# Values' products of an attention kernel, divided over the two row halves of the array

## The chip, the cores and the metric

The kernel runs on one core of a Trainium2 chip. The core has five engines, each with an instruction queue of its own that is worked off in order: TensorE (PE; its weight loads are shown apart, as PEld), VectorE (DVE), ScalarE (ACT), GpSimd (POOL) and SyncE (SP), which issues most of the DMAs. They wait for each other through semaphores. Matrix products are written to the eight banks of PSUM, 128 partitions by 512 float32 numbers each; everything else lies in SBUF. The metric is the device time of one execution in microseconds, and less is better.

## The reference

Two independent attentions over 2048 positions, model width 576, 32 heads of 18. A is local: every query sees itself and seven earlier positions, two apart. B is full softmax attention. Their outputs stand side by side in the result.

```python
qkv = (x @ wqkv).reshape(B, S, 3, H, Dh).transpose(2, 0, 3, 1, 4)
q, k, v = qkv[0], qkv[1], qkv[2]
# A: W, dil = 8, 2
logits = jnp.einsum("bhsd,bhswd->bhsw", q, kg) * scale      # kg, vg: eight gathered neighbours
o = jnp.einsum("bhsw,bhswd->bhsd", softmax(logits), vg)
# B
scores = jnp.einsum("bhqd,bhkd->bhqk", q, k) * scale
o = jnp.einsum("bhqk,bhkd->bhqd", softmax(scores), v)
# both
return o.transpose(0, 2, 1, 3).reshape(B, S, D) @ wo
```

## The kernel before

**Stages.** First come the projections of both attentions, then the main loop over B's attention with A's work strewn in, then a tail in which output projections are finished. TensorE's float32 inputs are split in a high and a low part where accuracy asks for it, so that projections are sums of several products.

**B's attention.** The heads are taken in 8 groups of 4 (NG = 8), the queries in 4 blocks of 512 (NB = 4), the keys in 16 steps of 128 (NT = 16). A step of the main loop (from "while step < ALL" on) handles 128 keys of 4 heads for 512 queries, and there are 8 x 4 x 16 = 512 steps. In a step `score` (lines 259 to 277) is called four times, for heads 0, 2, 1, 3. It multiplies 56 rows, in the upper half of the array's rows for heads 0 and 2 (r = 0) and the lower half for 1 and 3 (r = 1), into one score bank (L269), and ScalarE takes the exponential into a tile e in SBUF (L276). The product of e with the values is `weigh` (L736 to L742). It runs one step later: in step n, behind the four scores of step n, come the values of step n - 1. Each of the four heads has 18 value columns and a column of ones for the denominator, 19 columns; the four heads' results lie at partitions 0, 32, 64 and 96 of one bank, po, and add up there over the block's 16 steps.

**Maxima.** Softmax needs a bound of the scores. For blocks to come, the scores are computed in the other direction (queries on partitions) and VectorE takes maxima over the keys: `take` (the product, L158) and `reduce` (L166). The order of a step is written out by hand at the end of the kernel: half a maximum for r = 1, score 0, a maximum for r = 1, score 2, score 1, half a maximum for r = 0, score 3, a maximum for r = 0, then the values. In steps whose number is in `copied` the half maxima are left out.

**Banks.** Seven banks beside po are handed out by `bank` in rings. In the main loop the ring "scores" has banks 0 to 3 and serves the scores in turn; the ring "else" has banks 4, 5, 6 and serves the maxima. Sums of A's output projection (`sums_of_a`, `beside`, L1058) take one bank of either ring. A bank is used again when its last reader has ended.

**Tiles e.** There are eight, six in one pool and two in another, used in turn by `counted`; a tile is written again when the values' products that read it have ended.

**A block's end.** When the 16th step's values are issued, `finish` (L744) copies po to a tile o in SBUF: on ScalarE (L749) where the next step holds a sum of A (`producing`) or no maxima are left, else on VectorE (L752). From there, steps later and through `later`: the denominators go out by DMA on SP's queue (step +1), VectorE inverts them (+8, L777), they are spread by DMA, and GpSimd multiplies o with them (+20, L780) and splits it (+21, +22). `later` and `plan` fix the place in the program's order; when it runs, each engine decides by its queue and its waits. For the last group the tail does this in a shorter way (`shortly`), and for the very last block `closing` (L817) works on po in two halves of columns.

**A's attention** is done on GpSimd (L882, L886, L925 to L928), a little on VectorE and ScalarE, planned over the steps by `local`.

**The tail.** When the maxima are used up, values are weighed for two steps together (`paired`), and sums of B's output projection stand between.

The loop's order, cut to what the change touches:

```python
for h in (0, 2, 1, 3):
    es[h] = score(g, b, kt, h, ...)
    ...
if ready and (kt % 2 == 0 or not paired):
    weigh(ready.pop(0))
ready.append((g, b, kt, es))
```

Of the kernel before, what the change touches and what calls it, by code (L numbers as in the profile page):

```python
# [7 lines left out]
F32 = mybir.dt.float32  # L8
F32R = mybir.dt.float32r
BF16 = mybir.dt.bfloat16  # L10
AF = mybir.ActivationFunctionType
# [12 lines left out]
NT = S // 128  # L24
NB = S // 512
SCALE = DH ** -0.5
# [22 lines left out]
def ap(t, *dims):  # L49

    return bass.AP(tensor=t.tensor, offset=t.offset, ap=[list(t.ap[0])] + [list(d) for d in dims])


def rows(t, *dims):

    return bass.AP(tensor=t.tensor, offset=t.offset, ap=[list(d) for d in dims])
# [3 lines left out]
def two_attentions(ctx: ExitStack, tc, xa, wa, woa, xb, wb, wob, out):  # L60
# [5 lines left out]
    nc = tc.nc  # L66
# [6 lines left out]
    p_bank = ctx.enter_context(tc.tile_pool(name="p_bank", bufs=1, space=PSUM))  # L73
# [3 lines left out]
    rings = {"all": list(range(7)), "scores": [0, 1, 2, 3], "else": [4, 5, 6]}  # L77
    ring = "all"

    def bank(kind=None):  # L80
        r = rings[kind or ring]
        r.append(r.pop(0))
        return p_bank.tile([128, 512], F32, name=f"bank{r[-1]}")
# [11 lines left out]
    po = p_po.tile([128, 512], F32, name="po")  # L95
# [10 lines left out]
    step = 0  # L106
# [4 lines left out]
    def plan(start, pieces):  # L111
        for n, f in pieces:
            agenda[start + n].append(f)
# [100 lines left out]
    given = [0, 0]  # L214
# [44 lines left out]
    e_room = None  # L259
    counted = [-1]  # L260

    def score(g, b, kt, h, kind="scores", between=None):

        assert (g, b) in placed
        qs, ks = sets[g % 3]
        p, r = divmod(h, 2)
        ps = bank(kind)
        at = slice(64 * r, 64 * r + 56)
        nc.tensor.matmul(ps, ks[at, p, 128 * kt : 128 * kt + 128], qs[at, b, p], start=True, stop=True)  # L269
        if between:  # L270
            between()

        counted[0] += 1
        early = counted[0] % 8 < 6
        e = (e_room if early else work).tile([128, 512], F32, name="e", bufs=6 if early else 2)
        nc.scalar.activation(e, ps, AF.Exp, scale=SCALE)  # L276
        return e

    vs = {}

# [97 lines left out]
    with (tc.tile_pool(name="x", bufs=1, side="right") as xp,  # L378
# [4 lines left out]
        early = ExitStack()  # L383
# [98 lines left out]
        if True:  # L482
# [34 lines left out]
            for c in range(5):  # L517
                one, other = (load, nc.scalar.dma_start) if c % 2 == 0 else (nc.scalar.dma_start, load)
# [79 lines left out]
            for t in range(NT):  # L598
                ps = bank()
# [94 lines left out]
            for t in order[:4]:  # L694
                ps = bank()
# [23 lines left out]
            es = []  # L719
# [10 lines left out]
        step = 0  # L730
# [2 lines left out]

    work = ctx.enter_context(tc.tile_pool(name="work", bufs=1, reuse_waits="tile"))
    ring = "else"
    def weigh(*steps):  # L736
        for g, b, kt, es in steps:
            for i in range(4):
                nc.tensor.matmul(po[32 * i : 32 * i + 19], vs[g][:, kt, 19 * i : 19 * i + 19], es[i],  # L739
                                 start=kt == 0, stop=kt == NT - 1)  # L740
        if kt == NT - 1:
            finish(g, b)  # L742

    def finish(g, b):  # L744
        o = work.tile([128, 512], F32, name="o", bufs=2)
        if g == NG - 1 and b == NB - 1:
            return closing(b, o, work.tile([128, 512], F32, name="rec", bufs=1))
        if step + 1 in producing or sum(given) == total:
            nc.scalar.activation(o, po, AF.Copy)  # L749
        else:  # L750

            nc.vector.tensor_copy(o, po)  # L752
            copied.add(step + 1)
        den = work.tile([128, 16], F32, name="den", bufs=2)
        rec = work.tile([128, 512], F32, name="rec", bufs=1)
        parts = []

        def room():
            if g == NG - 1 and b == 0:

                parts[:] = [ap(work.tile([128, 4, 128], F32R, name=f"at{i}", bufs=1), (1, 512)) for i in range(2)]
            else:
                n = work.tile([128, 2, 512], F32R, name="n", bufs=1)
                parts[:] = n[:, 0], n[:, 1], n
            return parts

        if g == NG - 1 and b > 0:
            return shortly(b, o, rec, *room()[:2])

        def store():  # L770
            if g < NG - 1:
                load(do[:, g, :, 512 * b : 512 * b + 512].rearrange("i p n -> p i n"), parts[2].bitcast(F32))
            else:
                plan(step, full(b, parts))

        for at, f in ((1, lambda: load(den, o[DH:128:32])),
                      (8, lambda: nc.vector.reciprocal(den, den)),  # L777
                      (9, lambda: load(drec[g, b].rearrange("i (p n) -> (i p) n", n=16), den)),
                      (13, lambda: load(rec, rows(drec[g, b], (512, 4), (0, 32), (1, 512)))),
                      (20, lambda: nc.gpsimd.tensor_mul(o, o, rec)),  # L780
                      (21, lambda: nc.gpsimd.tensor_copy(room()[0], o)),
                      (22, lambda: nc.gpsimd.tensor_sub(parts[1], o, parts[0])),
                      (26, store)):
            later(at, f)

    def shortly(b, o, rec, hi, lo):

        def halved(cols):
            nc.gpsimd.tensor_copy(hi[:, cols], o[:, cols])
            nc.gpsimd.tensor_sub(lo[:, cols], o[:, cols], hi[:, cols])  # L790


        cols = [slice(256 * i, 256 * i + 256) for i in range(2)]
        apart = b == 1
        for i in range(2):
            later(1 + i * apart, lambda i=i: nc.vector.transpose(rec[:, cols[i]], o[:, cols[i]]))
        later(1 + 2 * apart, lambda: divided(rec))
        for i in range(2):
            later(1 + (3 + i) * apart, lambda i=i: nc.vector.transpose(o[:, cols[i]], rec[:, cols[i]]))
            later(1 + (3 + i) * apart, lambda i=i: halved(cols[i]))  # L800
        plan(step, [(at + 2, f) for at, f in full(b, (hi, lo))])

    def inverse(src, turned, cols, o):

        nc.vector.transpose(turned[:, cols], src[:, cols])
        divided(turned[:, cols])
        nc.vector.transpose(o[:, cols], turned[:, cols])
# [9 lines left out]
    def closing(b, o, rec):  # L817

        n = work.tile([128, 2, 512], F32R, name="n", bufs=1)
        first(3, b, 1)  # L820
        for t in range(4):
            if t % 2 == 0:
                inverse(po, rec, slice(128 * t, 128 * t + 256), o)
            cols = slice(128 * t, 128 * t + 128)
            hi, lo = n[:, 0, cols], n[:, 1, cols]
            nc.scalar.activation(hi, o[:, cols], AF.Copy)
            nc.gpsimd.tensor_sub(lo, o[:, cols], hi)
        for t in range(4):
            end(t, b, (n[:, 0], n[:, 1]))
# [4 lines left out]
    producing = set()  # L834
# [322 lines left out]
    early = sum(given)  # L1157
    rest = NG * NB * PIECES * 2 - early

    total = early + rest  # L1160
# [4 lines left out]
    while step < ALL:  # L1165
        n, kt = divmod(step, NT)
        g, b = divmod(n, NB)
        es = [None] * 4
# [4 lines left out]
        ps = bank() if inside and whole else None  # L1173
# [60 lines left out]
```

## Time and profile before

| | |
|---|---|
| time, median of 3 runs | 1605.34 us (1602.68 to 1605.59) |
| span of the profiled execution | 1603.8 us |
| TensorE, VectorE, ScalarE, GpSimd busy | 1590.0, 1383.7, 1217.7, 960.1 us |
| granted clock of TensorE, mean | 0.998 |
| 4096 records of the values' products (L739) | 537.7 us busy |
| 2048 records of the scores (L269) | 568.9 us busy |
| 2048 exponentials (L276) | 1049.9 us busy |
| 2048 maxima (L166) | 1288.3 us busy |

The runs' times are of unprofiled executions; the span is that of the one that was profiled, from its first to its last instruction. Busy time counts overlapping instructions of an engine once. In the profile a line such as L739 is a line of the kernel; "po<-e,v" names the tile that is written and those that are read; "128*19 128x512" on TensorE means 128 rows of the array, 19 columns, 512 numbers streamed. "x8" is a count. In the groups, the two numbers after the bar are the busy time in us and the mean duration in ns, then comes the engine's idle time before such instructions and what ended it. In a timeline the columns are start and duration in us; a row with a count reaches from the first start to the last end. Ends of matmuls are modelled.

### The profile page before, as it was taken

The numbers are of one execution on the slowest core, as the hardware profiler recorded it, in microseconds if no ns is written. First come the engines' busy times: TensorE is split into PE (matmuls) and PEld (weight loads), VectorE is DVE, ScalarE is ACT, GpSimd is POOL, SyncE is SP. The second block draws the span as 40 slices with busy tenths as digits, with TensorE's granted clock in tenths as the row PEclk, the third lists the DMA queues.
The fourth block names the chain that finished last, engine by engine and source line by source line (L and its number), as shares of the span: only waits on it lengthen the run. The fifth ranks groups of instructions, "written<-read, shape, count | busy, mean of one in ns | idle before, by whom it ended". The sixth has DMA issues, their size and how long they took to land.

```text
span 1603.8 us, 35232 instructions
## 1 busy us (share of the span) xinstructions
PE 1590.0 (99%) x13388; PEld 950.3 (59%) x13388; DVE 1383.7 (86%) x2347; ACT 1217.7 (76%) x2438; POOL 960.1 (60%) x792
## 2 busy tenths in 40 slices
PE   9999999999999999999999999999999999999998
PEld 7999888999543444444444444444444444445676
DVE  5299899999999999999999999999999999999512
ACT  6423441221699999999999999999999999898655
POOL 2405742201166995896797897797797797772100
PEclk9999999999999999999999999999999999999999
DMA  8937954522312362254326325422632231144111
GB/s 247 235 125 199 258 173 124 162 92 80 74 37 67 72 143 72 59 133 99 73 76 143 74 78 131 105 78 61 135 100 65 65 96 32 50 163 157 62 39 60
DMA packets 186058, 172.11 MB, mean 107 GB/s; under 512 B 119152, under 2 KB 132976, under 8 KB 184160
## 3 DMA queue, kind: packets, MB, share of 16 engines
q1 hardware_dynamic: 181024, 158.31, 36.1%
q0 software_dynamic: 4032, 10.63, 3.1%
q8 instruction: 105, 1.72, 0.5%
q10 hardware_dynamic: 832, 0.92, 0.2%
q14 instruction: 65, 0.53, 0.1%
HBM read 96.94 MB, written 71.90 MB: 105 GB/s over the span
## 4 chain that ended last, share of the span: by engine, by line
PE 91%; DVE 4%; DMA 2%; ACT 2%; issue 0%; POOL 0%; SPq 0%; POOLq 0%; DVEq 0%; ACTq 0%
PE po L739 29%; PE bank L269 18%; PE bank L158 17%; PE bank L361 15%; PE bank L1058 8%; PE bank L298 5%; DVE mx L166 3%; ACT e L276 1%; DMA dqk<-olo 1%; DMA dqk<-ohi 1%; DMA den<-o 0%; POOL xlo L409 0%; PE bank L513 0%; DVE as L900 0%; ACT lg L909 0%
## 5 line engine op out<-in xcount | busy, mean ns | idle before, releaser
L166 DVE TENSOR_REDUCE mx<-bank 128x2 f32<-128x512 f32 x2048 | 1288.3, 684 | 110.5 <-PE bank L158 82.6
L276 ACT ACTIVATE e<-bank 128x512 f32<-128x512 f32 x2048 | 1049.9, 608 | 46.6 <-PE bank L269 43.3
L158 PE MATMUL bank<-ks,qs 54*128 54x256 f32 (+1 forms) x2530 | 787.7, 378 | 4.2 <-DVE mx L166 2.5
L158 PEld LDWEIGHTS bank<-ks,qs 54*128 54x128 f32 x2530 | 408.8, 184 | 445.7 <-DVE mx L166 397.0
L269 PE MATMUL bank<-qs,ks 56*128 56x512 f32 x2048 | 568.9, 426 | 0.0
L739 PE MATMUL po<-e,v 128*19 128x512 f32 x4096 | 537.7, 599 | 0.0
L269 PEld LDWEIGHTS bank<-qs,ks 56*128 56x128 f32 x2048 | 299.7, 184 | 29.3 <-ACT e L276 25.2
L882 POOL TENSOR_TENSOR pr<-aq,akv 128x1024 f32<-128x1024 f32 x72 | 158.3, 2200 | 15.8 <-DMA akv<-da 13.0
L925 POOL TENSOR_TENSOR pr<-lg,akv 128x1024 f32<-128x1024 f32 x72 | 158.3, 2199 | 0.6
L886 POOL TENSOR_TENSOR pr<-pr 128x1024 f32<-128x1024 f32 x64 | 152.6, 2384 | 5.0
L739 PEld LDWEIGHTS po<-e,v 128*19 128x19 f32 x4096 | 70.5, 97 | 129.1 <-issue 123.6
L689 ACT ACTIVATE ohi<-bank 128x512 f32<-128x512 f32 (+1 forms) x56 | 30.4, 595 | 150.8 <-issue 104.2
L361 PE MATMUL bank<-xhi,ahi 64*128 64x512 f32 (+1 forms) x448 | 114.3, 387 | 0.0
L361 PE MATMUL bank<-xhi,alo 64*128 64x512 f32 (+1 forms) x448 | 109.6, 387 | 0.0
L361 PE MATMUL bank<-xlo,ahi 64*128 64x512 f32 (+1 forms) x448 | 105.8, 388 | 0.1
L926 POOL TENSOR_TENSOR pr<-pr 128x512 f32<-128x512 f32 x72 | 92.4, 1284 | 5.6
L409 POOL TENSOR_TENSOR alo<-raw,ahi 128x512 fp32r<-128x512 f32 (+1 forms) x14 | 17.6, 1255 | 121.4 <-ACT ahi L408 113.2
L501 POOL TENSOR_TENSOR olo<-olo,ohi 128x512 fp32r<-128x512 f32 x36 | 46.2, 1294 | 70.9 <-ACT ohi L500 62.8
L101 POOL CAST mh<-mt 128x32 fp32r<-128x32 f32 x32 | 6.7, 210 | 101.5 <-DVE mt L183 96.3
L361 PEld LDWEIGHTS bank<-xhi,ahi 64*128 64x128 f32 (+1 forms) x448 | 64.1, 182 | 4.4
L499 ACT ACTIVATE olo<-bank 128x512 f32<-128x512 f32 x36 | 21.2, 589 | 56.4 <-PE bank L361 31.4
L361 PEld LDWEIGHTS bank<-xhi,alo 64*128 64x128 f32 (+1 forms) x448 | 60.2, 182 | 4.4
(203 smaller groups left out, 1846.2 us busy)
## 6 DMA issues: line engine op xcount, KB each, us to landing
do<-n SPq DMA_DIRECT2D x28, 512.0 KB
da<-ohi SPq DMA_DIRECT2D x52, 256.0 KB
akv<-da SPq DMA_DIRECT2D x64, 175.5 KB
out<-y SPq DMA_DIRECT2D x32, 288.0 KB
qs<-dqk SPq DMA_DIRECT2D x30, 288.0 KB
ks<-dqk SPq DMA_DIRECT2D x30, 288.0 KB
at<-dao SPq DMA_DIRECT2D x60, 128.0 KB
rec<-drec SPq DMA_DIRECT2D x29, 256.0 KB
```

Source lines behind the costliest of these rows:

```text
L158: return nc.tensor.matmul(ps if part is None else ps[:, 256 * r : 256 * r + 256], qs[at, b, p, 128 * t : 128 * t + 128], ks[at, p, 512 * k ...
L166: nc.vector.tensor_reduce(at, ps.rearrange("q (s n) -> q s n", s=2), axis=AX.X, op=ALU.max)
L269: nc.tensor.matmul(ps, ks[at, p, 128 * kt : 128 * kt + 128], qs[at, b, p], start=True, stop=True)
L276: nc.scalar.activation(e, ps, AF.Exp, scale=SCALE)
L298: nc.tensor.matmul(ps, a, b, start=c == i == 0, stop=c == 4 and i == 1)
L361: nc.tensor.matmul(ps, a, b, start=start, stop=stop)
L739: nc.tensor.matmul(po[32 * i : 32 * i + 19], vs[g][:, kt, 19 * i : 19 * i + 19], es[i], start=kt == 0, stop=kt == NT - 1)
L882: nc.gpsimd.tensor_mul(pr, ap(st["q"][:, 2 * c], (SUB, 2), (0, W), (1, SUB)), window(st["k"], c))
L886: nc.gpsimd.tensor_add(st["pr"], st["pr"], pr)
L925: nc.gpsimd.tensor_mul(at, ap(st["lg"], (0, 2), (SUB, W), (1, SUB)), window(st["v"], c))
L926: nc.gpsimd.tensor_add(at[:, :, :4], at[:, :, :4], at[:, :, 4:])
L1058: nc.tensor.matmul(ps, a, b, start=start, stop=stop)
```

## The change

Every values' product over 128 keys is divided in two products of 64 keys, one in either half of the array's rows. The upper half's results add up in po, the lower half's in a second bank, po2, which is bank 3 of the score ring; three banks are left for the scores. At a block's end ScalarE copies po2 to a tile taken from the e tiles' turn, VectorE copies po, and GpSimd adds the two. The very last block adds them with VectorE, half by half.

```diff
@@ in score
+        e = room_of_e()
+        nc.scalar.activation(e, ps, AF.Exp, scale=SCALE)
+        return e
+
+    def room_of_e():
         counted[0] += 1
         early = counted[0] % 8 < 6
-        e = (e_room if early else work).tile([128, 512], F32, name="e", bufs=6 if early else 2)
-        nc.scalar.activation(e, ps, AF.Exp, scale=SCALE)
-        return e
+        return (e_room if early else work).tile([128, 512], F32, name="e", bufs=6 if early else 2)
@@ before the main loop
+    rings["scores"].remove(3)
+    po2 = p_bank.tile([128, 512], F32, name="bank3")
+    nc.vector.memset(po2, 0.0)
+
     def weigh(*steps):
         for g, b, kt, es in steps:
             for i in range(4):
-                nc.tensor.matmul(po[32 * i : 32 * i + 19], vs[g][:, kt, 19 * i : 19 * i + 19], es[i],
-                                 start=kt == 0, stop=kt == NT - 1)
+                for r, to in enumerate((po, po2)):
+                    at = slice(64 * r, 64 * r + 64)
+                    nc.tensor.matmul(to[32 * i : 32 * i + 19], vs[g][at, kt, 19 * i : 19 * i + 19], es[i][at],
+                                     start=kt == 0, stop=kt == NT - 1)
@@ in finish
-        if step + 1 in producing or sum(given) == total:
-            nc.scalar.activation(o, po, AF.Copy)
-        else:
-
-            nc.vector.tensor_copy(o, po)
+        other = room_of_e()
+        nc.scalar.activation(other, po2, AF.Copy)
+        nc.vector.tensor_copy(o, po)
+        if not (step + 1 in producing or sum(given) == total):
             copied.add(step + 1)
+        nc.gpsimd.tensor_add(o, o, other)
@@ in closing
         for t in range(4):
             if t % 2 == 0:
-                inverse(po, rec, slice(128 * t, 128 * t + 256), o)
+                both = slice(128 * t, 128 * t + 256)
+                nc.scalar.activation(o[:, both], po2[:, both], AF.Copy)
+                nc.vector.tensor_add(o[:, both], po[:, both], o[:, both])
+                inverse(o, rec, both, o)
```

## The prediction

> **What bounds the kernel now.** I read the page first, for the engines and the chain that ended last.
>
> ```profile
> span 1603.8 us, 35232 instructions
> ...
> PE 1590.0 (99%) x13388; PEld 950.3 (59%) x13388; DVE 1383.7 (86%) x2347; ACT 1217.7 (76%) x2438; POOL 960.1 (60%) x792
> ...
> PE 91%; DVE 4%; DMA 2%; ACT 2%; issue 0%; POOL 0%; SPq 0%; POOLq 0%; DVEq 0%; ACTq 0%
> ```
>
> TensorE looks like the only bound, but its ends are modelled, so I ask the stages. Columns: us, then busy us of PE, PEld, DVE, ACT and POOL, then granted clock and DMA.
>
> ```profile
> 700.00:1000.00 300.00, 299.57 (x2473) 139.29 (x2474) 280.94 (x480) 285.82 (x566) 246.37 (x176) 1.00 0.42 100
> 1500.00:1604.00 104.00, 97.82 (x1106) 72.60 (x1098) 23.22 (x55) 56.45 (x122) 4.48 (x10) 0.99 0.12 44
> ```
>
> In the attention stage ScalarE is 95% busy, VectorE 94%, GpSimd 82%: three engines stand beside TensorE, at a full clock, so time freed on TensorE alone is worth little there unless the others can follow. Only the last hundred microseconds are TensorE's alone. Next, one step of the loop (128 keys of 4 heads) in the timeline, a row for each group.
>
> ```profile
> 801.41 0.63 PE L739 MATMUL po<-e,v 128*19 128x512 f32 x4
> 801.85 0.61 PE L739 MATMUL po<-e,v 128*19 128x512 f32 x4
> 802.36 0.62 ACT L276 ACTIVATE e<-bank 128x512 f32<-128x512 f32 x1
> 802.39 0.38 PE L158 MATMUL bank<-ks,qs 54*128 54x256 f32 x1
> 802.40 0.50 PE L269 MATMUL bank<-qs,ks 56*128 56x512 f32 x1
> 802.93 0.60 ACT L276 ACTIVATE e<-bank 128x512 f32<-128x512 f32 x1
> 803.03 0.18 PEld L269 LDWEIGHTS bank<-qs,ks 56*128 56x128 f32 x1
> 803.08 0.46 PE L269 MATMUL bank<-qs,ks 56*128 56x512 f32 x1
> 803.10 0.43 PE L158 MATMUL bank<-ks,qs 54*128 54x512 f32 x1
> 803.47 0.63 PE L739 MATMUL po<-e,v 128*19 128x512 f32 x4
> 804.45 0.38 PE L158 MATMUL bank<-ks,qs 54*128 54x256 f32 x1
> ```
>
> Values at 801.41 and again at 803.47: a step is 2.06 here. A float32 values' product shows as two records, so the four products are eight: four at 801.41, four at 801.85. Two joints are idle. The last maximum starts at 803.10 and the values only at 803.47, 0.37 later; the values start at 803.47 and the next score phase at 804.45, 0.98 later. The first joint is seen in the waits too:
>
> ```profile
> PEld po L739 <- issue: 110.9, 452, 0.3
> PEld bank L269 <- ACT e L276: 22.8, 43, 0.8
> ```
>
> 452 times, 0.25 us each, a weight load of the values waited for nothing that the profile names: the array emptying between 128-row and 64-row products. The second thing to see is the fourth score of the step (803.08). Its weight load stands at 803.03, just after the exponential that ended at 802.36 + 0.62 = 802.98: that one frees the score bank which the ring of four gives it. The loop is tied to ScalarE through the banks.
>
> **The change part by part.**
>
> *Products in halves.* Eight products (sixteen records) of 64 rows by 19 columns replace four of 128 by 19. Does the joint go? The page has no 64x19 product, but one neighbour: the last projection chunk runs 64 rows by 64 columns among 64-by-128 maxima.
>
> ```profile
> 419.29 0.39 PE L361 MATMUL bank<-xhi,ahi 64*64 64x512 f32 x1
> 419.30 0.39 PE L361 MATMUL bank<-xhi,alo 64*64 64x512 f32 x1
> 419.52 0.39 PE L158 MATMUL bank<-ks,qs 54*128 54x512 f32 x1
> 419.53 0.39 PE L361 MATMUL bank<-xhi,ahi 64*64 64x512 f32 x1
> ```
>
> Both halves take their next product 0.23 after the last, whatever its width. So with equal row height I expect no joint: values 0.23 after the last maximum in place of 0.37. The two halves I take to run at once, as those pairs do, and the eight value tiles at 0.44 a pass (801.41 to 801.85), two passes, 0.88, and 0.02 for eight starts instead of four (four add 0.63 - 0.61): 0.90 in place of 0.98. Then the next score's load is hidden too, which shows as 0.39 instead of 0.50 in its duration:
>
> ```profile
> 801.07 0.39 PE L269 MATMUL bank<-qs,ks 56*128 56x512 f32 x1
> ```
>
> That saves 0.14 + 0.08 + 0.11 = 0.33 us of TensorE a step. Bounds: nothing, if the joints stay, to 0.33.
>
> *Three score banks.* The fourth score of a step now takes the bank of the first score of the same step. It must wait for that score to be computed and its exponential to end, and matmuls behind it in TensorE's queue (the last maximum, then the values, then the next step) wait with it. So a loop closes within one step. From the rows: first exponential at 802.93, ends 803.53; bank to matmul 0.10 (802.98 to 803.08): 803.63. Today it stands at 803.08. Last maximum 0.02 later (803.08 to 803.10): 803.65; values 0.23 after it: 803.88; next first score 0.90 after them: 804.78; 0.39 for the score and 0.03 to the exponential (802.40 + 0.50 to 802.93): 805.20. **The step is 805.20 - 802.93 = 2.27 us.** The saving of the first part is in it. What a step takes now:
>
> ```profile
> 800.92 30.57 ACT L276 ACTIVATE e<-bank 128x512 f32<-128x512 f32 x60 [0.80 <-PE bank L269]
> 831.34 0.63 ACT L749 ACTIVATE o<-po 128x512 f32<-128x512 f32 x1
> 831.82 1.63 ACT L276 ACTIVATE e<-bank 128x512 f32<-128x512 f32 x3
> ```
>
> Fifteen steps in 30.57: 2.04. So +0.23. How many steps: all exponentials, less those of the tail, by four.
>
> ```profile
> L276 ACT ACTIVATE e<-bank 128x512 f32<-128x512 f32 x2048 | 1049.9, 608 | 46.6 <-PE bank L269 43.3
> ...
> L276 ACT ACTIVATE e<-bank 128x512 f32<-128x512 f32 x110 | 57.4, 610 | 13.5 <-PE bank L269 13.4
> ```
>
> (2048 - 110) / 4 = 484 steps: 484 x 0.23 = **+111**. Each of the 32 half-sums of local attention also takes a bank of the ring, before the fourth score, and so meets the same wait; I count those steps alike. Bounds for the step: 2.20 (bank to matmul 0.03 shorter, no 0.02, scores 0.02 quicker) to 2.35 (0.08 more at the eight tiles): +77 to +150.
>
> *The end of a block.*
>
> ```profile
> L749 ACT ACTIVATE o<-po 128x512 f32<-128x512 f32 x23 | 14.6, 635 | 1.6 <-PE po L739 1.6
> L752 DVE COPY o<-po 128x512 f32<-128x512 f32 x8 | 5.5, 681 | 0.0
> L780 POOL TENSOR_TENSOR o<-o,rec 128x512 f32<-128x512 f32 x29 | 37.3, 1286 | 6.7 <-DMA rec<-drec 6.7
> L777 DVE RECIPROCAL den<-den 128x16 f32<-128x16 f32 x29 | 7.0, 242 | 0.6 <-DMA den<-o 0.6
> ```
>
> ScalarE copies the second bank after every block (31 times, where it copied 23), VectorE the first (31 times, where it copied 8), GpSimd adds them (31 new, 1.29 each by L780's row). ScalarE's copy waits for the last values, which end 0.17 (0.61 - 0.44) after the next score phase begins; the copy then keeps ScalarE 0.48 (831.34 to 831.82), and the next first exponential, which is ready 0.42 after its score started, begins about 0.17 + 0.05 + 0.48 - 0.42 = 0.3 late, on the loop. The room for its copy is one of the eight e buffers, so the buffers shift by one: the fourth exponential of the next step must wait for the values of this step, which end when that step is over, and pushes the exponential after it by the same 0.3. So 0.6 for 28 blocks of the main stage, **+17** (bounds 0 and 31). VectorE's 23 copies of 0.68, 16 us, hide: it idles 2.27 - 1.9 a step (281 of 300 busy at 2.04). Without that cover they would cost 16.
>
> *The wait on GpSimd.* Two steps after a block's end the fourth exponential takes the buffer of that copy, and waits for the add; behind it stands all of ScalarE. Counted from the first score of the step that holds the block's last values: these end at 2.27 + 0.17, ScalarE's copy at 3.1 (0.63). The next two steps begin at 2.57 and 5.15; in the latter the fourth score comes 0.42 + 0.70 in, its exponential 0.42 later, at 6.7. So the add has to start by 5.4. GpSimd works in strings:
>
> ```profile
> 831.19 2.21 POOL L882 TENSOR_TENSOR pr<-aq,akv 128x1024 f32<-128x1024 f32 x1
> 833.49 2.39 POOL L886 TENSOR_TENSOR pr<-pr 128x1024 f32<-128x1024 f32 x1
> 835.96 2.21 POOL L882 TENSOR_TENSOR pr<-aq,akv 128x1024 f32<-128x1024 f32 x1
> ```
>
> A pair ahead of the add, 4.6, makes it end at 3.1 + 4.6 + 1.3 = 9.0, 2.3 late; mostly less is ahead, since the slower steps give GpSimd more room. I take 0.35 a block, **+10** (bounds 0 and 28 x 2.3 = 64). The load of the denominators, one step later on SP, waits for the add as well, and holds SP's later loads; its reader (L777) comes seven steps, 16 us, later, so nothing. Were that cover gone, a late add would stop VectorE by up to the same 2.3.
>
> *The tail.* 110 exponentials are 27 steps without maxima.
>
> ```profile
> 1571.27 0.73 PE L269 MATMUL bank<-qs,ks 56*128 56x512 f32 x4
> 1571.84 0.30 PE L1058 MATMUL bank<-qs,wohi 62*128 62x288 f32 x2
> 1571.87 2.06 ACT L276 ACTIVATE e<-bank 128x512 f32<-128x512 f32 x4 [2.05 <-PE bank L269]
> ```
>
> Here the sum of products starts right behind the scores, at 1571.84. With three banks the fourth score comes at 1571.87 + 0.60 + 0.10 = 1572.57 and the sum behind it: +0.75. 27 x 0.75 = 20, less 0.33 for each of 13 pairs of values, 4: **+16** (bounds 5, if half of it falls into waits, and 20). *Closing:* two copies and two adds of 256 columns on the way to the end; the nearest row is a transpose of that size on VectorE at 0.45, so four would be 1.8, partly side by side: **+1.5** (0 to 1.8). Clearing the second bank once: 0.7 at most, hidden.
>
> Sum: 111 + 17 + 10 + 16 + 1.5 = 155.5. On the span, 1603.8 + 155.5 = 1759.3; the median of the runs, 1605.3, stands 1.5 above that span: **1761 us**. Its own range: 1705 (77, and half of each smaller term, 22) to 1830 (150, 31, 27 for GpSimd, 16, 1.5).
>
> **Rivals.**
>
> *The joints stay.* If a change between 64x32 and 64x128 empties the array as 128x32 and 64x128 do now, the 0.33 comes back, and 0.02 with it: step 2.62, +0.58, 484 x 0.58 = 281; with 17, 10, 20 and 1.5: 1605 + 329 = **1935**. For it: 452 waits of 0.25. Against: the 64*64 rows. The Trainium skill's page "TensorEngine Tiling (Array Packing)", section "Tiling Modes", says that a change of tiling mode, not just of tile, drains TensorE, and it lists 64x64 and 64x128 as two modes; the rows at 419.29 to 419.53 don't show that drain, the 0.25 waits do. By that rule this rival would be the forecast.
>
> *The halves take turns.* If two value tiles in one column strip can't stream together, values take 1.76 instead of 0.88: +0.88 x 512 on top, above **2150**. Against: every 64-row pair on the page runs side by side.
>
> *Faster.* If the exponential gives its bank up when it has read it rather than when it ends, the loop within the step opens. It decides where the fourth score can start 0.47 after the first exponential instead of 0.70 (0.23 less: the step is back at 2.04). Then ScalarE sets the pace: a pass over a bank keeps it 0.48 (831.34 to 831.82), four are 1.92; (2.04 - 1.92) x 484 = 58 off, 28 back: **1575**. Against it the row at 803.03, 0.05 after the end of its exponential, and 43 waits on ACT.
>
> **How the numbers follow.** Forecast 0.62; joints stay 0.20; halves take turns 0.05; faster 0.10; no change to be told, 0.03, where the loop's excess and the savings cancel. The range, 1700 to 1940, holds the first two (0.82). About 0.2% is what a measurement of this kernel can tell from no change. Slower 0.87, same 0.03, faster 0.10.
>
> **What would show it.** The values' first record 0.23 behind the last maximum, and the waits put to "issue" gone: the halves work; at 0.37, the first rival. Sixteen records within 0.9: the halves run together. The fourth score's load just behind the end of the first exponential of its own step, with TensorE idle some 0.5 before it, named as waiting for ACT: the loop. ScalarE's busy share of the stage at 1.92 / 2.27, 85%. Exponentials that wait for GpSimd two steps after a block, and how long. The forecast is wrong if the fourth score stands within 0.5 of the first exponential's start.

## The result, and the profile after

| | before | after |
|---|---|---|
| time, median (4 runs each) | 1604.65 us | 1909.25 us (1908.89 to 1909.78) |
| ratio | | 1.1901, interval 1.1884 to 1.1917 |
| span of the profiled execution | 1603.8 us | 1907.2 us |
| first exponential of the main loop | 416.9 us | 414.2 us |
| 484 steps with maxima, from first exponential to first exponential | 1064.5 us | 1349.9 us |
| one of these steps, median | 2.043 us | 2.626 us |
| the 27 steps without maxima | 107.5 us | 125.7 us |
| last of these exponentials to the end | 15.0 us | 17.4 us |

The lower five rows are worked out from the exponentials' starts in the two traces. The step took 0.583 us more where 0.23 was forecast: 484 x 0.583 = 282 of the 303 us by which the span grew. First the page after: the span, the engines, the chain that ended last.

```profile
span 1907.2 us, 43535 instructions
...
PE 1724.1 (90%) x17484; PEld 968.8 (51%) x17484; DVE 1407.8 (74%) x2373; ACT 1238.5 (65%) x2448; POOL 996.6 (52%) x823
...
PE 76%; ACT 17%; issue 2%; DMA 2%; DVE 1%; POOL 1%; SPq 0%; POOLq 0%; ACTq 0%; DVEq 0%
```

No engine is full any more, and ScalarE has 17% of the chain where it had 2%: work is passed back and forth between TensorE and ScalarE. The same stage of 300 us as before, in the windows (us, then busy us of PE, PEld, DVE, ACT, POOL, then clock and DMA):

```profile
700.00:1000.00 300.00, 265.33 (x2816) 117.17 (x2800) 226.80 (x386) 228.65 (x446) 205.57 (x154) 1.00 0.34 80
```

Every engine has lost busy share, at a full clock. Next one step in the timeline; of the sixteen records of values the first and the last of each pass are shown.

```profile
862.62 0.50 PE L269 MATMUL bank<-qs,ks 56*128 56x512 f32 x1
...
863.16 2.06 ACT L274 ACTIVATE e<-bank 128x512 f32<-128x512 f32 x4 [0.56 <-PE bank L269]
...
863.81 0.50 PE L269 MATMUL bank<-qs,ks 56*128 56x512 f32 x1 [0.32 <-ACT e L274]
...
863.81 0.50 PE L158 MATMUL bank<-ks,qs 54*128 54x512 f32 x1
...
864.24 0.09 PEld L748 LDWEIGHTS po<-e,v 64*19 64x19 f32 x1 [0.25 <-issue]
864.24 0.60 PE L748 MATMUL po<-e,v 64*19 64x512 f32 x1
...
864.29 0.60 PE L748 MATMUL bank<-e,v 64*19 64x512 f32 x1
...
864.68 0.59 PE L748 MATMUL po<-e,v 64*19 64x512 f32 x1
...
864.73 0.59 PE L748 MATMUL bank<-e,v 64*19 64x512 f32 x1
...
865.25 0.18 PEld L158 LDWEIGHTS bank<-ks,qs 54*128 54x128 f32 x1 [0.85 <-DVE mx L166]
```

The row that names bank 3 ("bank<-e,v") is the product into po2. Read it as four links that add up to the step. First exponential to fourth score: 863.16 to 863.81, 0.65, of which the exponential itself is 0.60 and 0.05 the way back to TensorE, which stands idle for 0.32. Fourth score to values: 863.81 to 864.24, 0.43, and their weight load waited 0.25 for nothing that is named, as before the change. Values to the next first score: 864.24 to 865.25, 1.01. That score to its exponential: 862.62 to 863.16, 0.54. Together 2.63. The waits of the whole run say the same (total us, times, longest); after:

```profile
PEld bank L269 <- ACT e L274: 281.4, 512, 1.1
...
PE bank L269 <- ACT e L274: 155.7, 461, 0.7
PEld po L748 <- issue: 127.9, 523, 0.3
```

and two of the same rows for the whole run before (the prediction's rows, 110.9 and 22.8 us, are those of a part of the main loop):

```profile
PEld po L739 <- issue: 123.6, 504, 0.3
...
PEld bank L269 <- ACT e L276: 25.2, 47, 0.8
```

After an exponential the weight load waited 47 times before, and the matmul itself never; now nearly every step has both (512 and 461 times). The wait put to "issue", the array emptying ahead of the values, should have gone and is as it was: about one in every step, 0.24 us each. What did not come is in the groups (busy, mean ns of one, then the idle time before them and what ended it):

```profile
L274 ACT ACTIVATE e<-bank 128x512 f32<-128x512 f32 x2048 | 1060.3, 604 | 280.7 <-PE bank L269 259.0 <-PE bank L748 12.8 <-PE bank L158 8.4
...
L762 POOL TENSOR_TENSOR o<-o,e 128x512 f32<-128x512 f32 x31 | 39.6, 1279 | 250.6 <-DVE o L759 210.1 <-ACT e L758 30.7 <-DVE mt L183 9.7
```

Exponentials hardly wait for GpSimd: the three releasers named, all TensorE, account for all but 0.5 of the 280.7 us. The 31 adds of a block's end took 1.28 each, as costed, and GpSimd was idle ahead of them: it waited for the copies, not the copies' buffer for it.

### The profile page after: what moved, and what is told of

It reads as the page before. It is cut to its first block, busy times and chain, and to the rows that moved or that the text cites. A ratio compares the mean times of both kernels' runs of the same rounds, so it can differ in the third digit from the quotient of the medians.

```text
span 1907.2 us, 43535 instructions
## 1 busy us (share of the span) xinstructions
PE 1724.1 (90%) x17484; PEld 968.8 (51%) x17484; DVE 1407.8 (74%) x2373; ACT 1238.5 (65%) x2448; POOL 996.6 (52%) x823
## 4 chain that ended last, share of the span: by engine, by line
PE 76%; ACT 17%; issue 2%; DMA 2%; DVE 1%; POOL 1%; SPq 0%; POOLq 0%; ACTq 0%; DVEq 0%
PE po L748 25%; PE bank L269 16%; ACT e L274 16%; PE bank L158 12%; PE bank L364 11%; PE bank L1070 7%; PE bank L301 4%; PE bank L748 1%; POOL xlo L412 1%; DMA raw<-xa 1%; DMA qs<-dqk 1%; DVE mx L166 1%; DMA dqk<-olo 0%; PE bank L516 0%; ACT y L1092 0%
## 5 line engine op out<-in xcount | busy, mean ns | idle before, releaser
L274 ACT ACTIVATE e<-bank 128x512 f32<-128x512 f32 x2048 | 1060.3, 604 | 280.7 <-PE bank L269 259.0
L158 PE MATMUL bank<-ks,qs 54*128 54x256 f32 (+1 forms) x2530 | 892.2, 392 | 1.3 <-DVE mx L166 0.8
L269 PE MATMUL bank<-qs,ks 56*128 56x512 f32 x2048 | 683.6, 442 | 156.5 <-ACT e L274 155.7
L158 PEld LDWEIGHTS bank<-ks,qs 54*128 54x128 f32 x2530 | 428.9, 184 | 444.1 <-DVE mx L166 392.6
L748 PE MATMUL po<-e,v 64*19 64x512 f32 x4096 | 546.3, 595 | 0.0
L748 PE MATMUL bank<-e,v 64*19 64x512 f32 x4096 | 546.1, 595 | 0.0
L762 POOL TENSOR_TENSOR o<-o,e 128x512 f32<-128x512 f32 x31 | 39.6, 1279 | 250.6 <-DVE o L759 210.1
L748 PEld LDWEIGHTS po<-e,v 64*19 64x19 f32 x4096 | 79.3, 93 | 127.9 <-issue 127.9
L748 PEld LDWEIGHTS bank<-e,v 64*19 64x19 f32 x4096 | 79.2, 93 | 0.1
L1070 PE MATMUL bank<-wohi,at 64*128 64x288 f32 x480 | 58.8, 304 | 14.2 <-ACT e L274 13.9
```

The costliest lines, as they stand in the source:

```text
L158: return nc.tensor.matmul(ps if part is None else ps[:, 256 * r : 256 * r + 256], qs[at, b, p, 128 * t : 128 * t + 128], ks[at, p, 512 * k ...
L748: nc.tensor.matmul(to[32 * i : 32 * i + 19], vs[g][at, kt, 19 * i : 19 * i + 19], es[i][at], start=kt == 0, stop=kt == NT - 1)
L1070: nc.tensor.matmul(ps, a, b, start=start, stop=stop)
```

## The experiments

All times are on the chip; a step is the median over the main loop. Three more medians recur. Two are between starts of TensorE records: **in**, from the last maximum of a step to the first value product; **out**, from the last value record to the next product. The third is **next**, the modelled duration of the first score behind the values, which is 0.50 where its weight load is exposed and 0.39 where it is hidden. Kernels without a ratio ran once. Those with 57 or 76 columns add several heads up in the same partitions, so they don't compute B's attention and are there for the times alone.

| kernel | time, us | ratio (interval) | step | in | out | next |
|---|---|---|---|---|---|---|
| before | 1604.65 | | 2.043 | 0.332 | 0.523 | 0.496 |
| after | 1909.25 | 1.190 (1.188 to 1.192) | 2.626 | 0.427 | 0.519 | 0.496 |
| three banks, values whole | 1891.66 | 1.179 (1.177 to 1.181) | 2.601 | 0.428 | 0.523 | 0.496 |
| halves in bfloat16 | 1766.36 | | 2.21, at two clocks | 0.429 | 0.360 | 0.498 |
| 57 columns float32, two places | 2356.59 | | 3.500 | 0.428 | 0.519 | 0.496 |
| 57 columns float32, one place | 3220.07 | | 5.191 | 0.427 | 0.519 | 0.496 |
| 76 columns float32 | 3058.57 | | 4.858 | 0.333 | 0.025 | 0.797 |
| 76 columns float32r | 1775.22 | 1.107 (1.105 to 1.109) | 2.349 | 0.332 | 0.223 | 0.392 |
| 57 columns float32r | 1776.42 | | 2.350 | 0.332 | 0.223 | 0.392 |
| first head with 256 queries | 1786.52 | 1.114 (1.111 to 1.116) | 2.381 | 0.427 | 0.519 | 0.383 |
| values in two places | 2230.55 | 1.391 (1.388 to 1.393) | 3.286 | 0.437 | 0.519 | 0.496 |
| whole, bfloat16, four banks | 1573.68 | 0.981 (0.979 to 0.983) | 2.000 | 0.376 | 0.898, a wait for VectorE | 0.496 |

The 0.332 of before and the 0.33 of the kernels in float32r are not the same thing. Before, the last maximum's load is hidden (its modelled duration is 0.40) and the way into the values holds the joint. In the float32r kernels that load is exposed (0.49), as in after, and the joint is what is missing: the wait of the values' loads put to "issue", 523 times in after, is there once.

### One part alone: three score banks

From before; nothing else is changed, bank 3 stays unused.

```diff
     ring = "else"
+    rings["scores"].remove(3)
```

> The kernel before with three score banks and nothing else changed: values' products stay whole, in one bank. Theory (the fourth score waits for the first exponential of its own step, and the idle stretch between scores and values is there with whole and with divided products): a step of 2.62 us, as with the change, and about 1900 us in all, which is the change's 1909 less some 8 for block ends and closing. Rival 1 (dividing the products saved something that the banks then ate up): slower than 1909, by up to 0.33 us a step, 160 us. Rival 2 (the divided products themselves cost most of it): at most 1750.

1891.66 us, 288 more than before measured beside it (1603.70). Its waits:

```profile
PEld bank L269 <- ACT e L276: 277.0, 498, 1.0
...
PE bank L269 <- ACT e L276: 158.2, 474, 0.6
PEld po L740 <- issue: 126.5, 515, 0.3
```

The missing bank alone brings 288 of the 305 us, with the same three waits. So dividing the products is worth nothing here, it costs: from 2.601 to 2.626, 0.025 us a step, 12 us in all, and some 5 more in the rest. Whether it is worth something beside four score banks, with po2 taken from the banks of the maxima, was not run.

### Halves with e and the values in bfloat16

From after; e, the values and their store in DRAM become BF16, and the copy of the second bank keeps float32.

```diff
-    dv = dram.tile([NG, 128, NT, 4 * 19], F32, name="dv")
+    dv = dram.tile([NG, 128, NT, 4 * 19], BF16, name="dv")
@@ room_of_e, load_v, v2: likewise
```

> The change with exponentials and values kept in bfloat16, so that a values' product is one record, not two (part of the precision is left out). Read from the trace is the stretch from the last maximum's start to the first value's start. Theory (the array empties whenever products of 19 columns follow or precede products of 128 columns, whatever their type): 0.42 us as with the change, and again an exposed weight load behind the values; step about 2.0 us, time about 1610. Rival (float32 products, and not their width, empty the array): 0.23 us, no exposed load, step about 1.92 where ScalarE sets it, time about 1570.

The values take one pass instead of two. The clock fell in this kernel, so its time, 1766.36, is not to be compared as it stands, and the step's median mixes two kinds: of the 484 steps, 234 took 1.95 to 2.10 us and 140 took 2.70 to 2.80. The shorter ones, with a median of 2.00, are 0.63 below after: the values' time lies on the loop. Their "in" is 0.43 as in after, so the joint isn't float32's alone, nor that of two passes. The fall of the clock in a window:

```profile
420.00:600.00 180.00, 175.28 (x1038) 86.58 (x1039) 134.02 (x217) 137.27 (x264) 101.09 (x84) 0.51 0.20 44
```

The clock is the third number from the end: 0.51 in this stretch; its mean over the kernel is 0.861.

### Is the joint a matter of columns, or of type?

The scores and the maxima are products of round float32 (F32R in the code, float32r below) with 128 columns; the values are float32 with 19. TensorE's rows print f32 for both types. Type and width differ, so three kernels widen the values' products. From after, in the first:

```diff
-                    nc.tensor.matmul(to[32 * i : 32 * i + 19], vs[g][at, kt, 19 * i : 19 * i + 19], es[i][at],
-                                     start=kt == 0, stop=kt == NT - 1)
+                    j = i // 2
+                    nc.tensor.matmul(to[64 * j : 64 * j + 57], vs[g][at, kt, 19 * j : 19 * j + 57], es[i][at],
+                                     start=kt == 0 and i % 2 == 0, stop=kt == NT - 1 and i % 2 == 1)
```

> The change with values' products of 57 columns instead of 19, two heads of a pair adding up in the same partitions (the attention of B is not computed rightly; it is there for the width alone). Products stay float32 and in halves; two follow each other in each column half, so values take twice as long. Read from the trace is the stretch from the last maximum's start to the first value's start. If only widths of up to 32 columns empty the array, 0.23 us and a step of about 3.2 us; if every float32 product or every width but 128 does, 0.42 us and a step of about 3.5 us.

In the second all 76 columns are taken, for every head at the same place:

```diff
+                    nc.tensor.matmul(to[:76], vs[g][at, kt], es[i][at],
+                                     start=kt == 0 and i == 0, stop=kt == NT - 1 and i == 3)
```

> The change with every values' product over all 76 columns of its group, so that it has the tile of the scores, 64 rows by 128 columns, and stays float32; the four heads of a step add up in the same partitions (B's attention is not computed rightly; it is there for the tile). Products now follow each other, four a half, some 3.5 us a step. Told apart by the first score behind the values, which lasts 0.50 us where its weight load is exposed and 0.39 us where it is hidden, and by the stretch from the last value's record to the next load. Theory now (a change of type between float32 and the scores' round float32 empties the array, whatever the tile): 0.50 us and 0.52 us. Rival (a change of width does): 0.39 us and about 0.45 us.

And in the third, e and the values are F32R besides (the copy of the second bank stays float32):

```diff
-    def room_of_e():
+    def room_of_e(dtype=F32R):
...
-        return (e_room if early else work).tile([128, 512], F32, name="e", bufs=6 if early else 2)
+        return (e_room if early else work).tile([128, 512], dtype, name="e", bufs=6 if early else 2)
...
-        vs[g] = (work if g % 2 else maxes).tile([128, NT, 4 * 19], F32, name="v", bufs=1)
+        vs[g] = (work if g % 2 else maxes).tile([128, NT, 4 * 19], F32R, name="v", bufs=1)
```

> As the run with 76 columns, but with exponentials and values in round float32, the type of the scores, so that neither the tile nor the type changes between scores and values; a product is one pass, four a half take about 0.88 us, as long as the change's values (precision is left out too). If a change of type or of tile empties the array, both ends are quick: first score behind the values 0.39 us, and the step is the forecast's 2.27 us, the time about 1909 - 484 x 0.35 = 1740. If something else empties it (the order, a wait, the second bank): 0.50 us and a step of 2.6 us, 1909.

With 57 columns the joint is as in after: 0.428, 0.519, 0.496. With 76 columns of float32 it is gone, although the type still changes. The timeline there, into the values and out of them:

```profile
1002.36 0.59 PE L748 MATMUL po<-e,v 64*76 64x512 f32 x1
1002.38 0.68 PE L158 MATMUL bank<-ks,qs 54*128 54x256 f32 x1
...
1003.87 0.50 PE L158 MATMUL bank<-ks,qs 54*128 54x512 f32 x1
1004.21 0.59 PE L748 MATMUL bank<-e,v 64*76 64x512 f32 x1
```

The next step's maximum is issued 0.02 behind the last value product, while that pass still streams; "out" and "next" (0.025 and 0.797) are therefore not to be read as in the other rows, but their sum is that pass, 0.43, and a score whose load is hidden, 0.39. The values come 0.34 behind the last maximum, of which 0.11 is the exposed load of that maximum (0.50 instead of 0.39). The step is long only because four heads now come one after another in two passes each. So **the type falls, the columns stand.**

With 76 columns of float32r a product takes one pass, and four in a row take no longer than the four side by side did. This is the loop as I had forecast it, without joints:

```profile
1000.85 0.50 PE L269 MATMUL bank<-qs,ks 56*128 56x512 f32 x1 [0.30 <-ACT e L274]
...
1001.19 0.39 PE L748 MATMUL bank<-e,v 64*76 64x512 f32 x1
...
1002.12 0.39 PE L269 MATMUL bank<-qs,ks 56*128 56x512 f32 x1
...
1002.55 1.58 ACT L274 ACTIVATE e<-bank 128x512 fp32r<-128x512 f32 x3 [0.28 <-PE bank L269]
...
1003.20 0.49 PE L269 MATMUL bank<-qs,ks 56*128 56x512 f32 x1 [0.32 <-ACT e L274]
```

The four links are 0.34 (1000.85 to 1001.19), 0.93 (to 1002.12), 0.43 (to 1002.55) and 0.65 (to 1003.20): 2.35. Forecast were 0.25, 0.90, 0.42 and 0.70: 2.27. The joint's price is the difference to after, 2.626 - 2.349 = 0.277 us a step: about 0.09 ahead of the values, 0.08 behind them, 0.11 for the load of the next score, which is exposed when the array has emptied. Over 484 steps it is 134 us. The time of this kernel (1775.22) lies 134.03 below that of after; by the exponentials' starts 128.5 of it come in the 484 steps and 5.1 in the 27 behind them.

### Why the 64*64 rows showed no joint

My forecast had rested on rows of 64 rows by 64 columns between maxima, without a joint. They are products of split parts, which are F32R in the code. Two kernels with 57 columns at partitions 0 to 56, in float32r and in float32:

```diff
+                    nc.tensor.matmul(to[:57], vs[g][at, kt, :57], es[i][at],
+                                     start=kt == 0 and i == 0, stop=kt == NT - 1 and i == 3)
```

> As the run with 76 columns in float32r, but with 57 columns, at partitions 0 to 56 of either bank (each head's product takes the first 57 value columns, and the four heads are summed there). Here the type is that of the scores and only the columns fall below 65. If a float32r product keeps the scores' column tile whatever its width, there is no joint: from the last maximum to the values 0.33 (with the exposed load), from the last value record to the next score phase about 0.22, the next score 0.39, step 2.35, time about 1775. That would also explain the 64*64 rows of the forecast. If the number of columns alone decides, the joint is there: 0.43, 0.50 for the next score, step 2.35 + 0.28 = 2.63, about 1910; then the 64*64 rows stay unexplained.

> The same 57 columns at the same place, but e and the values in float32, as a mate to the run with 57 columns in float32r and to the one with 76 columns in float32 (step 4.86, no joint: 0.33 into the values, 0.025 out). If fewer than 65 columns in float32 are put in a smaller column tile, the joint is there: 0.43 into the values, 0.50 for the next score, step 4.86 + 0.28 = 5.14, time about 3190. If what brought the joint in the kernel after the change was the place (heads at partitions 32, 64, 96) and not the width, then 0.33 and step 4.86, about 3060.

The timeline of the first, out of the values and into the next:

```profile
1001.09 0.39 PE L748 MATMUL bank<-e,v 64*57 64x512 f32 x1
1001.32 0.39 PE L269 MATMUL bank<-qs,ks 56*128 56x512 f32 x1
...
1002.40 0.49 PE L158 MATMUL bank<-ks,qs 54*128 54x512 f32 x1
1002.73 0.40 PE L748 MATMUL bank<-e,v 64*57 64x512 f32 x1
```

And of the second:

```profile
1001.09 0.50 PE L158 MATMUL bank<-ks,qs 54*128 54x512 f32 x1
1001.52 0.63 PE L748 MATMUL po<-e,v 64*57 64x512 f32 x1
...
1004.58 0.59 PE L748 MATMUL bank<-e,v 64*57 64x512 f32 x1
1005.10 0.38 PE L158 MATMUL bank<-ks,qs 54*128 54x256 f32 x1
```

Same shape, same place, one type apart: 0.23 out and 0.33 in with float32r, 0.52 and 0.43 with float32. (The step with float32 came out at 5.19, 0.05 above what I had set. Against the 76 columns it is 0.33 longer: 0.09 ahead of the values, 0.05 from their first record to their last, 0.19 from there to the next exponential.) So in these kernels a narrow product empties the array if it is float32 (or bfloat16, with 19 columns), and does not if it is float32r. That float32r products keep all 128 columns of the array, whatever their width, is the reading that fits; the runs show it by times alone. The Trainium skill's page "PSUM — Partial Sum Buffer", section "The four PSUM rules", says in passing that float32r matmuls force the full column group in the instruction, which agrees with it.

### Half of the first head's queries

From after, the loop's first link is shortened: head 0's scores, exponentials and values take 256 queries, and the other 256 of that head are left out.

```diff
-        nc.tensor.matmul(ps, ks[at, p, 128 * kt : 128 * kt + 128], qs[at, b, p], start=True, stop=True)
+        n = 256 if h == 0 else 512
+        nc.tensor.matmul(ps[:, :n], ks[at, p, 128 * kt : 128 * kt + 128], qs[at, b, p, :n], start=True, stop=True)
@@ the exponential and the products of head 0: likewise [:, :n]
```

> The change with head 0's scores, exponentials and values taken for the first 256 of 512 queries only (the rest of that head is left out). Theory (the loop runs from a step's first score through its exponential to the fourth score): the score ends 0.11 us sooner and the exponential 0.21 us sooner, the step falls from 2.62 to about 2.30 us, the time by about 155 us to about 1755. Rival (the step is bound by TensorE's own work or by another engine, and the wait only fills idle time): step and time as with the change, within 20 us.

2.381 and 1786.52, not 2.30 and 1755. The timeline of a step:

```profile
1001.58 0.38 PE L270 MATMUL bank<-qs,ks 56*128 56x256 f32 x1
...
1002.06 0.38 PE L158 MATMUL bank<-ks,qs 54*128 54x256 f32 x1
1002.08 0.87 ACT L275 ACTIVATE e<-bank 128x256 f32<-128x256 f32 x2 [0.52 <-PE bank L270]
...
1002.52 0.49 PE L270 MATMUL bank<-qs,ks 56*128 56x512 f32 x1
```

The fourth score still follows the first exponential, 0.05 behind its end (in this kernel's groups one of 256 queries has a mean of 0.384, against 0.604 of all after): the loop holds, and the step is 0.245 shorter through one head's work alone, 0.22 of it the exponential. But the exponential begins 0.50 behind the start of its score, hardly sooner than the 0.54 of after, though the score ends 0.12 earlier. In this kernel's trace ScalarE's empty instruction between the two half maxima (L249) stands ahead of it and comes at 1002.00, when the first half maximum is done; so I take it, and no longer the score, for what the exponential waits for, and for the 0.08 by which I missed; no run leaves that instruction out.

### The values in two places

From after, heads 0 and 1 are weighed between the second and the third score, heads 2 and 3 at the end.

```diff
+        split = ready and not paired
         for h in (0, 2, 1, 3):
+            if split and h == 1:
+                weigh(ready[0], heads=(0, 1))
...
-        if ready and (kt % 2 == 0 or not paired):
+        if split:
+            weigh(ready.pop(0), heads=(2, 3))
+        elif ready and (kt % 2 == 0 or not paired):
             weigh(ready.pop(0))
```

> The kernel after, but the values of a step stand at two places of the step's order: heads 0 and 1 between the second and the third score, heads 2 and 3 at the end. Nothing is left out. The theory: with three banks every score waits for the exponential three scores before it, and whatever stands in TensorE's order between a score and the next lengthens that loop. In the kernel after, first score to fourth score is 1.19 us, and fourth score to the next first score 1.44, of which the values are 0.9. With half of them moved out the loop is 1.19 + 1.44 - 0.44 = 2.19, and what then bounds a step is TensorE's own work with a second pair of joints, 2.2 to 2.4: with 2.3 the time is 1909 - 484 x 0.33 = 1750 (1700 to 1800). The rival, that the third bank costs a wait that doesn't depend on the order, keeps the wait and adds a pair of joints: 2.63 + 0.28 = 2.9, about 2040.

Both missed: 3.286 and 2230.55. The matmuls' wait that the change had brought is gone from the waits, though not the weight loads' row of that name:

```profile
PEld bank L269 <- ACT e L274: 427.3, 501, 1.0
...
PE bank L269 <- ACT e L274: 12.0, 21, 0.7
```

TensorE itself waited 12.0 us instead of 155.7, so the wait does depend on the order, and a fixed cost of the third bank is out. The 427.3 us are the 0.85 behind the first two heads' values in each step, in which the values still stream. But the timeline shows what I had overlooked:

```profile
862.05 0.60 PE L748 MATMUL po<-e,v 64*19 64x512 f32 x1
...
862.49 0.59 PE L748 MATMUL po<-e,v 64*19 64x512 f32 x1
...
863.03 0.50 PE L269 MATMUL bank<-qs,ks 56*128 56x512 f32 x1
...
863.69 0.60 PE L748 MATMUL po<-e,v 64*19 64x512 f32 x1
```

Two heads take 0.98 (862.05 to 863.03), nearly as long as four (1.01): a pass is 0.44 whether two or four heads share the columns. Parting them paid the whole of the values twice, not a half in each place; TensorE is 99% busy again, and its step is twice the way from 862.05 to 863.69, 2 x 1.64 = 3.28.

### A version that beats both

From before: four score banks, whole products, but e and the values in bfloat16, at that precision.

```diff
-        e = (e_room if early else work).tile([128, 512], F32, name="e", bufs=6 if early else 2)
+        e = (e_room if early else work).tile([128, 512], BF16, name="e", bufs=6 if early else 2)
@@ dv, v, v2: likewise
```

> The kernel before with exponentials and values in bfloat16 (part of the precision is left out): four score banks, whole products of 128 rows, one pass instead of two records each. Values take 0.22 us instead of 0.88. Theory (the step then hangs on ScalarE, four passes of 0.48 us): 1.92 to 1.95 us, 484 x 0.1 = 48 less, about 1555. Rival (the clock falls with the load, as the mean of 0.861 in the halves' bfloat16 run shows): scores at half clock, a step of 2.0 us or more, 1600 or slower.

1573.68 us, ratio 0.981. It gains 1.9%, not the 3% that I had set. The windows, in the order as above, and a group of the whole run (busy, mean ns of one, idle time before and what ended it) say why:

```profile
600.00:800.00 200.00, 160.56 (x1319) 94.33 (x1319) 191.42 (x333) 193.06 (x387) 156.97 (x121) 0.98 0.36 85
...
1000.00:1200.00 200.00, 158.53 (x1315) 92.82 (x1315) 190.49 (x324) 192.50 (x385) 178.14 (x134) 1.00 0.38 92
...
L158 PE MATMUL bank<-ks,qs 54*128 54x256 f32 (+1 forms) x2530 | 833.6, 395 | 191.5 <-DVE mx L166 186.6
```

TensorE is down to 80%, and ScalarE and VectorE are nearly full, 97% and 96% in the first stretch. I had counted ScalarE alone, 1.92 to 1.95 a step. The step is 2.00, and it hangs on VectorE: Ahead of its own products for the maxima TensorE stood idle for 186.6 us until VectorE had read a bank (379 waits), where before it was 2.5 us; VectorE's reductions have 31% of the chain that ended last, where they had 3%. Most steps hold three of them, 0.67 each where they follow on each other. The clock fell here too, to 0.974 in the mean, but it doesn't explain the step, which is 2.00 as well in the second stretch, at a clock of 1.00.

## Why the prediction was right or wrong

**Right: the direction and its mechanism.** The fourth score takes the first score's bank, follows its exponential by 0.05, and everything behind it in TensorE's queue waits along: a loop within each step. Three banks alone brought 288 of 305 us; one head's exponential shortened, the step shortened with it; float32r, where the joint is gone, gives 2.35 against the 2.27 forecast. The halves ran together, sixteen records in two passes 0.44 apart, so "the halves take turns" was wrong, and so was "faster": the score follows 0.05 behind the end of the exponential, not when the bank has been read. That 1909 lies in the range that I gave is owed to the first rival, which the range was made to hold; my sum alone reached 1830 at most.

**Wrong: "So with equal row height I expect no joint".** This step failed, and the rival "the joints stay" (step 2.62, 1935 us) is what happened (2.626, 1909). Equal row height isn't enough; float32 products of 19 columns and the scores' of 128, all in 64 rows, have a joint between them. The Trainium skill's page "TensorEngine Tiling (Array Packing)", section "Tiling Modes", says that changing the tiling mode drains TensorE; these runs agree, with 0.277 a step. The rows at 419.29 that I had set against it were float32r products, and those don't leave the scores' mode. I had looked at their shape and not at their type. The joint of 0.277 in 484 steps is 134 us of the miss of 148 (1909.25 - 1761).

**The loop itself: +111 forecast, +148 measured** (484 x (2.349 - 2.043)). The term left out is the weight load of the fourth score and of the last maximum: coming out of a wait they have nothing to hide behind, 0.50 instead of 0.39, and the values start some 0.1 later (0.34 instead of 0.25). The values themselves took 0.93 instead of 0.90. The way from exponential to matmul, 0.05 and not the 0.10 I took, gives 0.05 back.

**A block's end, +17, and GpSimd, +10: too large.** What the two steps at the blocks' ends cost beyond the median grew by 7.7 us in all, from 49.3 to 57.0 by the exponentials' starts; the other steps' excess fell by 4.5. Three banks alone, without copy and add, have 51.3 in the same steps, so the block's end and GpSimd together brought 5.7 us, where I had 27. Of the two 0.3 that I had put on a block's end, the first came as 0.22: the step that holds a block's last values takes 2.85, at each of the 30 block ends in the loop. The second, by the shifted buffer, hardly came: in 14 blocks the fourth exponential of the following step waited for the values (the 12.8 us put to L748 above), and that step is some 0.1 longer than the same step of other blocks. GpSimd's add was not late. (My range counted 27 for GpSimd where my own bound was 64; neither came.)

**The tail, +16, and closing, +1.5:** 18.2 and 2.4. The first exponential came 2.7 earlier, which I had not forecast and did not look into. Together: 285.4 for the steps, 18.2, 2.4 and -2.7 make 303.3 of the span's 303.4.

**The rival's sum** was 26 above the time although its step was exact to 0.01: it carried the same 17 and 10 for the block's end and GpSimd, where the steps beyond their medians brought 3.2 net (1349.9 - 1064.5 - 282.2): 24 too much.

## What to carry to other kernels

Before a joint is costed as gone, compare the tile of both neighbours in rows, in columns and in type; a row of the same shape and another type is no witness. When a ring of buffers gets shorter than the calls of one step, close the loop first, from a buffer's writer through its reader back to the next writer and on through that engine's queue: it sets the step, and whatever is gained elsewhere no longer counts, here not even the halved products. Work that shares the array side by side cost a pass of 0.44 here for two heads as for four, so it couldn't be parted for half the price.

## What the runs showed of the hardware that I had not expected

- **Type decides whether a narrow product empties the array:** 57 columns of float32r, 0.33 in and 0.22 out; the same in float32, 0.43 and 0.52.
- **Four float32r products in a row take no longer than four float32 products side by side:** 0.93 against 1.01 from the first value to the next score. Each is one record instead of two.
- **The clock fell under bfloat16 values:** means of 0.861 (halves) and 0.974 (whole), where before, after and all the kernels in float32 or float32r kept 0.996 or more in every run. In the halves it was 0.51 from 420 to 600 us, though TensorE was busy for 175.28 of those 180 us and its longest idle time by the records was 0.73 us. The cause stays open.
